# Second gated FFN with ScalarE, VectorE and GpSimd in written order instead of a scheduler's order

## The chip, the cores and the metric

The kernel runs on one NeuronCore of a Trainium2 chip. The metric is the device time of one execution in microseconds: 1541.91 us, the median of three runs (1540.91 to 1547.6). A profiled execution of the same kernel took 1539.89 us, of which the profile's span (first to last instruction) covers 1538.1 us.

## The reference

Three stages follow each other. The changed part is the last one.

```python
xread = softmax(x @ state.T / 8) @ state          # attention between 512 tokens and 32 states
sread = softmax(state @ x.T / 8) @ x              # per batch (8) and head (8), D = 64
x = concat([xread, sread]) -> rows of 512         # 8 * 544 = 4352 rows
x = ((x @ w1) * (x @ w2)) @ w3 @ w_out            # first FFN, 512 -> 1024 -> 512
out = (sigmoid(x @ w_gate) * (x @ w_val)) @ w_out2  # second FFN, 512 -> 1536 -> 512
```

The weights come as float64. The kernel reads their 32-bit words and builds float32 from them on the chip. Each float32 operand of a matrix product is split into a high part (rounded to the matmul's reduced fp32 format) and a low part (the rest), and three of the four cross products are summed.

## The kernel before

Everything up to `ffn1(B, ...)` (L633) is attention and the first FFN; its result goes to DRAM as `yd`, transposed, in five pieces of 7, 7, 7, 7 and 6 blocks of 128 rows. Then the pools are released and the second FFN starts.

The second FFN runs 15 steps: three passes over the hidden width (four tiles of 128 columns each, `JQ`), and in each pass the five row pieces. A step consists of two calls of `gate_val` (the halves q = 0 and q = 1), and the step's `down` product (hidden to 512 columns) runs inside the next step, so 14 + 14 products and one `down` belong to each step.

- `gate_val` computes gate and value with a fast 2x2 block scheme that needs 7 products in place of 8. Each of the 14 products (7 for gate, a = 0; 7 for value, a = 1) is six matmuls of 448 columns (384 in the piece of 6 blocks) into one PSUM bank. Tags: A (two banks, accumulated over products 1, 6, 5, 3 and read out in between to `s1`, `u2`, `u4` by ScalarE, `keep_`), B (two banks), C (one bank, product 2). `finish` adds a kept piece (VectorE), applies the sigmoid (ScalarE, gate) or multiplies gate and value (VectorE), and splits the product into `p` (high part on ScalarE, low part on VectorE).
- `down` runs, per block of 128 rows, twelve matmuls of 512 columns `po<-wo,p`, and evicts to `ob`; in passes 1 and 2 it adds the partial result `pr` of the pass before, read back from DRAM.
- `load_y` brings in the operands of the next step: per half of the 512 inputs two loads `yf`, four differences `yt`, seven splits into the 14 pairs `y` (high part ScalarE, low part VectorE). Sixteen pairs of buffers exist.
- `prep_next` prepares the weights of the next pass beside this work: 24 pieces per pass are loaded (`raw`, DMA issued by GpSimd), narrowed from float64 (`narrow`: two operations on ScalarE, four on VectorE), combined on GpSimd, split (`o`: ScalarE, then GpSimd), and stored to DRAM (`wd`, `wod`; GpSimd's queue, 36 stores per pass). Loads and store tiles share two buffers (tag `io`).

Only TensorE's order is written out by hand (L143). The other engines' instructions are put in order by a list scheduler, from a priority that follows the program text and from its own cost estimates; each engine then executes that order strictly, so an instruction that waits holds back all that stands behind it on its engine. `prep_step` hands the scheduler one piece of weight work per product (L833, L841) or per block of `down` (L856).

Of the kernel before, what the change touches and what calls it, by code (L numbers as in the profile page):

```python
# [20 lines left out]
def tile_state_attention__then__gated_ffns(  # L21
# [19 lines left out]
    nc = tc.nc  # L41
# [27 lines left out]
    def cvt(src, cv, nb=3):  # L69

        raw = cv.tile([P, 512, 2], U32, name="raw", bufs=nb)
        shape = list(src.shape)
        view = raw if len(shape) == 2 else raw.rearrange("p (k f) t -> p k f t", k=shape[1])
        flat = "p f t -> p (f t)" if len(shape) == 2 else "p k f t -> p k (f t)"
        nc.sync.dma_start(out=view.rearrange(flat), in_=src)  # L80
        m = cv.tile([P, 512], F32, name="m", bufs=nb)
        narrow(raw, m, cv.tile([P, 512], I32, name="r", bufs=2))
        return m

    def narrow(raw, m, r):
        hi, lo = raw[:, :, 1], raw[:, :, 0]
        mu = m.bitcast(U32)
        nc.scalar.activation(out=m, in_=hi.bitcast(F32), func=AF.Abs)  # L88
        nc.scalar.activation(out=r, in_=lo, func=AF.Copy, scale=2.0**-29)  # L89
        nc.vector.tensor_scalar_max(m, m, 2.0**-15)  # L90
# [52 lines left out]
    with tc.manual_schedule(engines={mybir.EngineType.PE}):  # L143
# [413 lines left out]

        ys = {}

        def load_y(c, cv):  # L560

            n = blocks[c] * P // 2
            ys[c] = [[None, None] for _ in range(7)]
            for kb in range(2):
                raw = []
                for h in range(2):
                    r = cv.tile([P, 2, 448 if cv is p2.get("c2") else 512], F32, tag="raw", name="yf", bufs=3)
                    nc.sync.dma_start(
                        out=r[:, :, :n], in_=y_d[c][2 * h + kb].rearrange("p (c n) -> p c n", c=2)
                    )  # L570
                    raw.append(r)
                b11, b12, b21, b22 = (r[:, i, :n] for r in raw for i in range(2))
                tt = [
                    cv.tile([P, 448 if cv is p2.get("c2") else 512], F32, tag="m", name="yt", bufs=3)[:, :n]
                    for _ in range(3)
                ]
                t1, t2, t3 = tt
                nc.vector.tensor_tensor(out=t1, in0=b12, in1=b11, op=ALU.subtract)
                nc.vector.tensor_tensor(out=t2, in0=b22, in1=t1, op=ALU.subtract)
                nc.vector.tensor_tensor(out=t3, in0=b22, in1=b12, op=ALU.subtract)  # L580
                t4 = b12
                nc.vector.tensor_tensor(out=t4, in0=b21, in1=t2, op=ALU.subtract)
                for o, v in enumerate((b11, t2, t3, t1, b21, b22, t4)):
                    t = [
                        p2["c1"].tile([P, 448], F32R, name=f"y{i}", bufs=16)[:, :n] for i in range(2)
                    ]
                    split(t[0], t[1], v)
                    ys[c][o][kb] = t
# [43 lines left out]
        slots[4].append(lambda: load_y(0, cv))  # L632
# [14 lines left out]
        p2["c2"] = c2  # L647
# [25 lines left out]
        def prep_next(ps):  # L673

            def load(src, k=None):
                raw = c2.tile([P, 256, 2], U32, tag="io", name="raw2", bufs=2)
                if k is None:
                    nc.gpsimd.dma_start(out=raw.rearrange("p f t -> p (f t)"), in_=src)  # L680
                else:
                    nc.gpsimd.dma_start(
                        out=raw.rearrange("p (k f) t -> p k (f t)", k=k), in_=src
                    )
                m = c2.tile([P, 256], F32, name="m2", bufs=4)
                narrow(raw, m, c2.tile([P, 256], I32, name="r2"))
                return m

            def put(dst, v):
                t = c2.tile([P, 2, 256], F32R, tag="io", name="o2", bufs=2)  # L690
                split(t[:, 0], t[:, 1], v, sub=nc.gpsimd)
                nc.gpsimd.dma_start(out=dst, in_=t.bitcast(F32))

            def chain(jp, a):
                m = {}
                j0 = 2 * jp
                dst = w_d[j0 + a].rearrange("p (o i f) -> o p i f", o=7, i=2)

                def get(jj, kb):
# [3 lines left out]
                    m[jj, kb] = load(w.rearrange("(k p) f -> p k f", p=P), k=2)  # L703

                def diff(o, x0, x1, op=ALU.subtract):
                    nc.gpsimd.tensor_tensor(out=o, in0=x0, in1=x1, op=op)

                def s1():
                    m["s"] = c2.tile([P, 256], F32, name="sm2")
                    diff(m["s"], m[1, 0], m[1, 1], ALU.add)  # L710
                    put(dst[2], m[1, 1])

                def s3():
                    put(dst[3], m["s"])
                    diff(m[1, 0], m[0, 0], m[1, 0])

                def s2():
                    put(dst[5], m[1, 0])
                    diff(m["s"], m["s"], m[0, 0])

                def s4():
                    put(dst[4], m["s"])
                    diff(m["s"], m[0, 1], m["s"])

                wo = wo_d[j0 + a].rearrange("p (i f) -> p i f", i=2)

                def out_half(h):
                    w = w_out2[(j0 + a) * P : (j0 + a + 1) * P, h * 512 : (h + 1) * 512]
                    m["o", h] = load(w)

                return [
                    lambda: get(1, 0), lambda: get(1, 1), lambda: get(0, 0), s1, s3,
                    lambda: get(0, 1), s2, lambda: put(dst[0], m[0, 0]), s4,
                    lambda: put(dst[1], m[0, 1]), lambda: put(dst[6], m["s"]),
                    lambda: out_half(0), lambda: put(wo[:, :, :256], m["o", 0]),
                    lambda: out_half(1), lambda: put(wo[:, :, 256:], m["o", 1]),
                ]

            return [chain(ps * 2 + q, a) for q in range(2) for a in range(2)] + [[]]

        todo2 = []

        def prep_step():
            if todo2:
                todo2.pop(0)()


        OPS = {1: (0, 0), 6: (4, 1), 7: (5, 2), 5: (3, 3), 2: (1, 4), 3: (6, 5), 4: (2, 6)}

        def gate_val(ps, c, q, between):  # L750
# [6 lines left out]
            def product(a, k, o, start):  # L757
                w, xx = OPS[k]
                w = wt[q, a][:, w]
# [22 lines left out]
            def finish(a, jj, cc, o, what):  # L782

                if a == 0:
                    t = c2.tile([P, 448], F32, name=f"sg{jj}{cc}")[:, :n]
                    if what is not None:
                        nc.vector.tensor_tensor(out=t, in0=o, in1=kept[a, what], op=ALU.add)  # L787
                        o = t
                    nc.scalar.activation(out=t, in_=o, func=AF.Sigmoid)  # L789
                    sg[jj, cc] = t  # L790
                    return
                t = sg[jj, cc]
                if what is not None:
                    nc.vector.tensor_tensor(out=kept[a, what], in0=o, in1=kept[a, what], op=ALU.add)  # L794
                    o = kept[a, what]
                nc.vector.tensor_tensor(out=t, in0=o, in1=t, op=ALU.mult)  # L796
                p = pt[2 * jp + jj]
# [140 lines left out]
```

## Time and profile before

| | before |
|---|---|
| median of three runs | 1541.91 us |
| profiled execution: time, span | 1539.89 us, 1538.1 us |
| busy in the span: TensorE, VectorE, ScalarE, GpSimd | 1380.0, 939.3, 748.1, 341.2 us |
| matmuls of the second FFN: first start, last end | 651.05 us, 1528.64 us |
| busy 722.5 to 1155.1 us: TensorE, VectorE, ScalarE | 386.99, 267.73, 205.41 of 432.6 us |
| busy 1155.1 to 1511.4 us: TensorE, VectorE, ScalarE | 351.44, 204.53, 132.82 of 356.3 us |

[...] A row of the timeline merges neighbouring instructions of one kind. The brackets give the idle time in front of it and what ended that. Buffer numbers are left out, so `raw2`, `m2`, `o2`, `s1`, `u2` of the code read `raw`, `m`, `o`, `s`, `u`.

### The profile page before, as it was taken

How to read it: one execution, taken by the hardware profiler on the slowest of the kernel's cores; microseconds unless marked ns; L12 is line 12 of the kernel's file. 1: busy time of each engine (PE TensorE's matmuls, PEld its weight loads, DVE VectorE, ACT ScalarE, POOL GpSimd, SP SyncE). 2: the span in 40 equal slices, each digit the busy share in tenths (PEclk: the TensorE clock that was granted, in tenths of full speed). 3: DMA queues.
4: the chain of work that ended last, by engine and by line, in shares of the span. 5: the costliest groups of instructions: out<-in, count | busy, mean ns of one | idle time of the engine just before them, and what ended most of it. 6: DMA issues, size and time to landing. Idle time of an engine off the chain costs nothing. (4 is left out here: it accounts for less than half of the span.)

```text
span 1538.1 us, 19065 instructions
## 1 busy us (share of the span) xinstructions
PE 1380.0 (90%) x6560; PEld 1160.7 (75%) x6560; DVE 939.3 (61%) x1639; ACT 748.1 (49%) x1480; POOL 341.2 (22%) x375
## 2 busy tenths in 40 slices
PE   5668999996999999859998998798989999999997
PEld 3347777774777878847787787687878888888886
DVE  7799767677745245328567466384674566457543
ACT  6666656755545445336446445263452354235321
POOL 2352123346412210032431422323310000000000
PEclk8789999998999999969999999899999999999999
DMA  8767647858523212462433338435433374341322
GB/s 259 249 183 205 177 156 220 255 187 260 186 82 96 62 61 80 166 269 94 166 133 103 130 136 305 174 117 177 159 104 107 132 267 157 98 128 57 107 96 69
DMA packets 155304, 237.18 MB, mean 154 GB/s; under 512 B 46920, under 2 KB 99656, under 8 KB 153160
## 3 DMA queue, kind: packets, MB, share of 16 engines
q1 hardware_dynamic: 132936, 169.38, 34.9%
q0 software_dynamic: 10752, 40.90, 7.6%
q10 hardware_dynamic: 11520, 25.70, 4.6%
q8 instruction: 51, 0.84, 0.2%
q14 instruction: 45, 0.37, 0.1%
HBM read 150.99 MB, written 84.93 MB: 153 GB/s over the span
## 5 line engine op out<-in xcount | busy, mean ns | idle before, releaser
L763 PE MATMUL psA<-y,wt 128*128 128x448 f32 (+1 forms) x1440 | 319.9, 371 | 39.0 <-ACT s L61 21.8
L763 PEld LDWEIGHTS psA<-y,wt 128*128 128x128 f32 x1440 | 273.6, 194 | 67.8 <-ACT s L61 28.0
L849 PE MATMUL po<-wo,p 128*128 128x512 f32 x1224 | 282.7, 391 | 2.2 <-ACT ob L61 1.9
L849 PEld LDWEIGHTS po<-wo,p 128*128 128x128 f32 x1224 | 230.4, 189 | 51.0 <-ACT ob L61 2.5
L763 PE MATMUL psB<-y,wt 128*128 128x448 f32 (+1 forms) x720 | 166.3, 367 | 16.9 <-DVE u L794 16.9
L109 PE MATMUL pab<-aT,swh 128*128 128x512 f32 x512 | 149.5, 415 | 23.0 <-ACT asb L61 12.3
L90 DVE TENSOR_SCALAR m<-m 128x512 f32<-128x512 f32 (+1 forms) x116 | 63.2, 549 | 159.5 <-ACT m L88 152.4
L763 PEld LDWEIGHTS psB<-y,wt 128*128 128x128 f32 x720 | 137.0, 193 | 28.5 <-DVE u L794 18.4
L67 POOL TENSOR_TENSOR swh<-swf,swh 128x512 fp32r<-128x512 f32 x64 | 89.4, 1399 | 241.9 <-ACT swh L61 225.1
L109 PEld LDWEIGHTS pab<-aT,swh 128*128 128x128 f32 x512 | 97.2, 197 | 48.5 <-ACT asb L61 14.5
L109 PE MATMUL py<-u,wp 128*128 128x512 f32 (+1 forms) x576 | 131.0, 380 | 0.0
L864 DVE TENSOR_TENSOR ob<-po,pr 128x512 f32<-128x512 f32 x68 | 46.8, 690 | 127.2 <-PE po L849 115.3
L109 PEld LDWEIGHTS py<-u,wp 128*128 128x128 f32 x576 | 103.4, 188 | 26.1 <-issue 6.4
L88 ACT ACTIVATE m<-raw 128x512 f32<-128x512 f32 (+1 forms) x116 | 65.9, 570 | 116.8 <-DMA raw<-in_moe_w_out 51.3
L431 DVE TENSOR_TENSOR asb<-asb,pab 128x512 f32<-128x512 f32 (+1 forms) x72 | 47.1, 655 | 102.3 <-PE pab L112 90.3
L763 PE MATMUL psC<-y,wt 128*128 128x448 f32 (+1 forms) x360 | 84.3, 370 | 18.4 <-DVE s L794 18.3
L61 ACT ACTIVATE p<-sg 128x448 fp32r<-128x448 f32 (+1 forms) x120 | 66.9, 563 | 58.9 <-DVE sg L796 57.9
L763 PEld LDWEIGHTS psC<-y,wt 128*128 128x128 f32 x360 | 67.0, 192 | 28.4 <-DVE s L794 24.2
L89 ACT ACTIVATE r<-raw 128x512 int32<-128x512 uint32 (+1 forms) x116 | 65.7, 566 | 44.0 <-DVE m L98 26.5
L789 ACT ACTIVATE sg<-psA 128x448 f32<-128x448 f32 (+1 forms) x30 | 15.7, 522 | 144.3 <-PE psA L763 144.3
L61 ACT ACTIVATE u<-psA 128x448 f32<-128x448 f32 (+1 forms) x120 | 63.0, 527 | 44.2 <-PE psA L763 43.1
L95 DVE SCALAR_TENSOR_TENSOR m<-raw,m 128x512 uint32<-128x512 uint32 (+1 forms) x116 | 81.6, 709 | 1.8
(128 smaller groups left out, 2194.5 us busy)
## 6 DMA issues: line engine op xcount, KB each, us to landing
raw<-in_moe_w SPq DMA_DIRECT2D x48, 512.0 KB, 5.1
yf<-yd SPq DMA_DIRECT2D x48, 448.0 KB, 3.5
wt<-wd SPq DMA_DIRECT2D x12, 1792.0 KB, 10.2
part<-ob SPq DMA_DIRECT2D x68, 256.0 KB, 2.0
pr<-part SPq DMA_DIRECT2D x68, 256.0 KB, 3.0
swd<-swst ACTq DMA_DIRECT2D x32, 512.0 KB, 3.8
swf<-swd SPq DMA_DIRECT2D x128, 128.0 KB, 3.0
wd<-o POOLq DMA_DIRECT2D x56, 256.0 KB, 3.0
```

What stands on the lines that cost most here:

```text
L61: nc.scalar.activation(out=o, in_=i, func=AF.Copy)
L67: (sub or nc.vector).tensor_tensor(out=lo, in0=src, in1=hi.bitcast(F32), op=ALU.subtract)
L88: nc.scalar.activation(out=m, in_=hi.bitcast(F32), func=AF.Abs)
L89: nc.scalar.activation(out=r, in_=lo, func=AF.Copy, scale=2.0**-29)
L90: nc.vector.tensor_scalar_max(m, m, 2.0**-15)
L95: nc.vector.scalar_tensor_tensor(out=mu, in0=hi, scalar=0xC0000000, in1=mu, op0=ALU.bitwise_and, op1=ALU.bitwise_or)
L109: nc.tensor.matmul(o, w[i], xx[k], start=n == 0 and i + k == 0, stop=False)
L431: nc.vector.tensor_tensor(out=asb[:, :n], in0=asb[:, :n], in1=pab[1][:, :n], op=ALU.mult)
L763: nc.tensor.matmul(o, w[:, i, kb * P : (kb + 1) * P], xx[kb][h], start=start, stop=i == 1 and kb == 1, skip_group_check=True,)
L789: nc.scalar.activation(out=t, in_=o, func=AF.Sigmoid)
L849: nc.tensor.matmul(o, pt[j][i][:, s * P : (s + 1) * P], wot[j][:, h], start=j == js[0] and i + h == 0, stop=j == js[-1] and i == 1,)
L864: nc.vector.tensor_tensor(out=ob, in0=o, in1=pr, op=ALU.add)
```

## The change

ScalarE, VectorE and GpSimd join TensorE in written order for the second FFN. TensorE's `gate_val` order stays, except that `down` now stands after three products of the first half and not after eight.

- A counter `now` goes up by one at every product and every half block of `down` (`begin`). Work that follows a product is put a fixed number of slots behind it (`later`): sigmoid and high parts two slots, low parts three.
- Token work (`next_tokens`, in place of `load_y`) is a list of 22 pieces with a condition each on the slot; `fill` hands out at most two splits per slot as long as a budget of VectorE time is positive.
- Weight work (`next_weights`, in place of `prep_next`) is a list of pieces handed out at least 2.0 us (of the planner's own clock) apart, from 10 us on. Its loads and stores are issued by ScalarE's queue instead of GpSimd's: the load of a piece at least 4.0 us ahead of its conversion, the store two slots behind the split. `raw2` gets one buffer of its own, `o2` two, `m2` three; the eight halves of `w_out2` tiles come last in a pass.
- The row `pr` of the next block is loaded one block ahead, and the pool's tiles are laid out in another order (four names more are allocated ahead of the weight tiles `wt`).

```diff
+        def later(k, cost, fn):
+            due.setdefault(clock["now"] + k, []).append((cost, fn))
+        def begin(length):
+            clock["now"] += 1
+            clock["us"] += length
+            clock["vector"] = min(clock["vector"] + length, 2.5)
+            for cost, fn in due.pop(clock["now"], []):
+                vector(cost)
+                fn()
+        def fill(quiet):
+            act = 0
+            if prep and clock["us"] >= clock["prep"]:
+                if not prep[0][0] or (
+                    quiet and clock["vector"] > -1.0 and clock["us"] >= clock["load"]
+                ):
+                    clock["prep"] = clock["us"] + 2.0
+                    act = 1
+                    clock["vector"] -= 1.5 * prep[0][0]
+                    for fn in prep.pop(0)[1:]:
+                        fn()
+            while tokens and clock["vector"] > 0.5 and act < 2 and tokens[0][0]():
+                _, is_split, fn = tokens.pop(0)
+                if is_split:
+                    act += 1
+                else:
+                    vector()
+                fn()
...
+                    copy("act", y[0], v)
+                    later(1, 0.62, lambda: (minus(y[1], v, y[0].bitcast(F32)), ready.add((c, o, kb))))
...
+            def load(src, k):
+                raw = c2.tile([P, 256, 2], U32, name="raw2")
+                nc.scalar.dma_start(out=raw.rearrange("p (k f) t -> p k (f t)", k=k), in_=src)
+                raws.append(raw)
+                clock["load"] = clock["us"] + 4.0
+            def conv(key):
+                raw = raws.pop()
+                m[key] = c2.tile([P, 256], F32, name="m2", bufs=3)
+                r = c2.tile([P, 256], I32, name="r2")
+                bits_act(raw, m[key], r)
+                later(1, 0.0, lambda: bits_vector(raw, m[key], r))
+            def put(dst, key):
+                t = c2.tile([P, 2, 256], F32R, name="o2", bufs=2)
+                split(t[:, 0], t[:, 1], m[key], sub=nc.gpsimd)
+                later(2, 0.0, lambda: nc.scalar.dma_start(out=dst, in_=t.bitcast(F32)))
...
                     nc.vector.tensor_tensor(out=t, in0=o, in1=kept[a, what], op=ALU.add)
+                    vector()
+                    later(2, 0.0, lambda: nc.scalar.activation(out=t, in_=t, func=AF.Sigmoid))
...
-                split(p[0][:, cc * n : (cc + 1) * n], p[1][:, cc * n : (cc + 1) * n], t)
+                later(2, 0.0, lambda: copy("act", hi, t))
+                later(3, 0.62, lambda: minus(lo, t, hi.bitcast(F32)))
...
-            for a, k in (
-                (0, 1), (1, 1), (0, 2), (0, 6), (1, 6), (0, 7), (0, 5), (1, 5),
-            ):
+            for a, k in ((0, 1), (1, 1), (0, 2)):
                 step(a, k)
-                if q:
-                    prep_step()
             between()
...
+        ordered = {mybir.EngineType.Activation, mybir.EngineType.DVE, mybir.EngineType.Pool}
+        with tc.manual_schedule(engines=ordered):
```

ScalarE at the start of the second FFN, the kernel before and then the changed one (`s`, `u` are read-outs of bank A, `m`, `r`, `o` weight work, `sg` the sigmoid):

```order
L88 ACTIVATE m_6218<-raw_6216 128x256
L89 ACTIVATE r_6219<-raw_6216 128x256
L88 ACTIVATE m_6237<-raw_6235 128x256
L89 ACTIVATE r_6238<-raw_6235 128x256
L61 ACTIVATE o_6275<-m_6237 128x256
L88 ACTIVATE m_6257<-raw_6255 128x256
L89 ACTIVATE r_6258<-raw_6255 128x256
L61 ACTIVATE o_6287<-sm_6273 128x256
L61 ACTIVATE s_6082<-psA 128x448
L61 ACTIVATE o_6320<-m_6218 128x256
```

```order
L61 ACTIVATE s_6016<-psA 128x448
L61 ACTIVATE s_6025<-psA 128x448
L61 ACTIVATE u_6046<-psA 128x448
L920 ACT_TABLE_LOAD
L920 ACTIVATE sg_6034<-sg_6034 128x448
L61 ACTIVATE u_6055<-psA 128x448
L61 ACTIVATE u_6070<-psA 128x448
L61 ACTIVATE u_6080<-psA 128x448
L920 ACTIVATE sg_6072<-sg_6072 128x448
L791 DMA raw_6090<-in_moe_w_gate 128x2x256
```

Before, eight operations of weight work that need landed loads stand ahead of the first read-out; in the changed kernel six read-outs and two sigmoids come first, and only then is the first weight load issued.

SP at the end of the first FFN, before and changed, with the semaphores that each DMA waits for (a `DMA...` semaphore is an earlier transfer; `wt`, `wo` are the second FFN's weights):

```order
L659 DMA wt_5981<-wd 128x3584 [waits DMASW0_49,PE_49]
L659 DMA wt_5983<-wd 128x3584 [waits DMAHW5_49,DMASW2_49]
L668 DMA wo_5985<-wod 128x1024 [waits DMAHW6_49,DMASW1_49,DVE_49]
L668 DMA wo_5987<-wod 128x1024 [waits DMAHW7_49,DMASW3_49,DVE_49]
L668 DMA wo_5989<-wod 128x1024 [waits DMAHW0_49,DMASW5_49]
```

```order
L711 DMA wt_5985<-wd 128x3584 [waits DMASW0_49]
L711 DMA wt_5987<-wd 128x3584 [waits DMAHW5_49,DMAHW6_49,DMASW2_49,DMAHW7_49,DVE_49,PE_49]
L720 DMA wo_5989<-wod 128x1024 [waits DMASW1_49,PE_49]
L720 DMA wo_5991<-wod 128x1024 [waits DMASW3_49]
L720 DMA wo_5993<-wod 128x1024 [waits DMAHW0_49,DMASW5_49,PE_49]
```

The first weight tile no longer waits for TensorE; the TensorE event of the second one lies 136 matmuls before the end of the first FFN (a `pab` product), where before the first tile waited for one that lies 20 before it (`py`).

VectorE in the second half of a step of pass 0, before and changed (`u`, `sg`: `finish` of the value; `yt`, `y`: token work):

```order
L794 TENSOR_TENSOR u_7482<-psB,u_7482 128x448
L582 TENSOR_TENSOR yf<-yf,yt 128x448
L67 TENSOR_TENSOR y_7050<-yt,y_7049 128x448
L67 TENSOR_TENSOR y_7054<-yt,y_7053 128x448
L67 TENSOR_TENSOR y_7058<-yt,y_7057 128x448
L67 TENSOR_TENSOR y_7062<-yf,y_7061 128x448
L796 TENSOR_TENSOR sg_7463<-u_7482,sg_7463 128x448
L67 TENSOR_TENSOR y_7066<-yf,y_7065 128x448
L67 TENSOR_TENSOR y_7070<-yf,y_7069 128x448
```

```order
L577 TENSOR_TENSOR y_7339<-yt,y_7338 128x448
L918 TENSOR_TENSOR sg_7354<-psB,u_7352 128x448
L924 TENSOR_TENSOR u_7362<-psB,u_7362 128x448
L927 TENSOR_TENSOR sg_7354<-u_7362,sg_7354 128x448
L577 TENSOR_TENSOR y_7377<-yf,y_7376 128x448
L577 TENSOR_TENSOR y_7389<-yt,y_7388 128x448
L577 TENSOR_TENSOR y_7392<-yt,y_7391 128x448
L577 TENSOR_TENSOR yt<-yf 128x448
L577 TENSOR_TENSOR yt<-yf,yt 128x448
L927 TENSOR_TENSOR sg_7394<-psA,sg_7394 128x448
```

Before, runs of token work stand inside a value's add and multiply; in the changed kernel the two stand next to each other and at most five token operations in a row stand between read-outs. From one add of bank C to the next (14 products) the fullest half has 23 tensor operations and one conversion of four on VectorE.

## Rows read from the trace of the kernel before

**Rows 1.** Busy time and granted clock by stretch (us, busy and count per engine, PEclk, DMA).
```profile
645.50:722.50 77.00, 51.34 (x217) 43.86 (x218) 39.26 (x81) 35.37 (x75) 21.17 (x29) 0.82 0.56 217
1155.10:1511.40 356.30, 351.44 (x1706) 315.02 (x1706) 204.53 (x364) 132.82 (x270) 0.00 (x0) 1.00 0.37 124
```
**Rows 2.** Waits of PE, 645 to 1538 us: in total, times, longest.
```profile
PE psA L763 <- ACT s L61: 21.8, 14, 7.8
PE psC L763 <- DVE s L794: 18.3, 15, 4.2
PE psB L763 <- DVE u L794: 16.9, 4, 9.0
```
**Rows 3.** Timeline of PE at the start of the second FFN.
```profile
644.36 1.12 PE L112 MATMUL py<-u,wp 128*128 128x256 f32 x8
651.05 2.61 PE L763 MATMUL psA<-y,wt 128*128 128x448 f32 x6 [5.57 <-DMA wt<-wd]
657.07 2.61 PE L763 MATMUL psA<-y,wt 128*128 128x448 f32 x6 [3.41 <-DMA wt<-wd]
```
**Rows 4.** Timeline and waits of SP, 615 to 660 us.
```profile
643.12 0.81 SPq L659 DMA_DIRECT2D wt<-wd  x2
...
SPq L659 <- PE py L109: 16.9, 1, 16.9
```
**Rows 5.** Chain that ended last, in order of time: pieces of pass 2.
```profile
1259.39 16.32 PE po L849 x72
...
1296.48 2.14 DVE y L67 x4
...
1306.86 1.22 PE psB L763 x6
...
1310.51 19.07 PE po L849 x84
...
1494.90 1.04 PE psC L763 x6
```
**Rows 6.** Timeline of PE: `down` of step 0, of step 7, the last.
```profile
722.47 16.48 PE L849 MATMUL po<-wo,p 128*128 128x512 f32 x72
...
1155.12 19.25 PE L849 MATMUL po<-wo,p 128*128 128x512 f32 x84
...
1513.92 14.72 PE L849 MATMUL po<-wo,p 128*128 128x512 f32 x63 [0.29 <-ACT p L61]
```
**Rows 7.** Timeline of ACT, then of PE, in step 6.
```profile
1058.03 0.43 ACT L88 ACTIVATE m<-raw 128x256 f32<-128x256 f32 x1 [5.87 <-DMA raw<-in_moe_w_out]
...
1059.44 2.61 PE L763 MATMUL psB<-y,wt 128*128 128x448 f32 x6 [3.91 <-DVE u L794]
```
**Rows 8.** ACT at the first two read-outs: timeline.
```profile
666.27 0.53 ACT L61 ACTIVATE s<-psA 128x448 f32<-128x448 f32 x1
...
676.73 0.53 ACT L61 ACTIVATE s<-psA 128x448 f32<-128x448 f32 x1
```
**Rows 9.** Instructions on the tile `raw`, 640 to 1200 us: who waited, landing times.
```profile
ACT m L88: 101.4, 35
...
DMA to landing us min/median/max: 2.8/3.4/10.3
```
**Rows 10.** The same for the tile `o`.
```profile
L67 POOL TENSOR_TENSOR o<-m,o x48: 717/736/2160, 659.9 to 1132.6; 128x256 fp32r<-128x256 f32 x48
...
ACT o L61: 70.5, 26
...
DMA to landing us min/median/max: 2.3/2.8/7.1
```
**Rows 11.** A DMA issued by ScalarE (first FFN), duration ns min/median/max.
```profile
L453 ACTq DMA_DIRECT2D yd<-ysb x48: 326/326/1496, 190.6 to 645.9; - x48
```
**Rows 12.** Timeline of DVE: first and last operation of one conversion.
```profile
675.25 0.29 DVE L90 TENSOR_SCALAR m<-m 128x256 f32<-128x256 f32 x1 [8.85 <-ACT m L88]
...
676.47 0.43 DVE L98 CUSTOM_DVE_ANT_0 m<-m,r 128x512 uint16<-128x512 uint16 x1
```
**Rows 13.** DVE by form, 700 to 980 us, then 1200 to 1460 us.
```profile
L67 DVE TENSOR_TENSOR p<-sg,p 128x448 fp32r<-128x448 f32 x28 | 17.5, 636 | 1.4 <-ACT p L61 1.2
...
L67 DVE TENSOR_TENSOR p<-sg,p 128x448 fp32r<-128x448 f32 x31 | 18.7, 619 | 6.5 <-ACT p L61 6.1
```

More of the change, by code (lines that the diff above doesn't have):

```diff
@@ L558, in tile_state_attention__then__gated_ffns, with y_tiles, y_raw @@
         ys = {}
-        def load_y(c, cv):
+        def y_tiles(n):
+            return [p2["c1"].tile([P, 448], F32R, name=f"y{i}", bufs=16)[:, :n] for i in range(2)]
+        def y_raw(c, kb, h, pool, w):
             n = blocks[c] * P // 2
-            ys[c] = [[None, None] for _ in range(7)]
-            for kb in range(2):
[L565 to L586, printed above, removed]
@@ L646, in tile_state_attention__then__gated_ffns, with vector @@
         tc.swap_default_side()
-        p2["c2"] = c2
+        clock = {"now": 0, "us": 0.0, "vector": 0.0, "prep": 10.0, "load": 0.0}
+        due = {}
+        tokens = []
+        prep = []
+        half = {}
+        ready = {(0, o, kb) for o in range(7) for kb in range(2)}
+        def later(k, cost, fn):
+            due.setdefault(clock["now"] + k, []).append((cost, fn))
+        def vector(cost=0.62):
+            clock["vector"] -= cost
+        def begin(length):
[23 more added lines that the diff above has]
+                fn()
         pt = {}
@@ L671, in load_wo @@
                 wot[j] = t
[L673 to L699, printed above, removed]
+        OPS = {1: (0, 0), 6: (4, 1), 7: (5, 2), 5: (3, 3), 2: (1, 4), 3: (6, 5), 4: (2, 6)}
@@ L702, in get @@
                     ]
-                    m[jj, kb] = load(w.rearrange("(k p) f -> p k f", p=P), k=2)
-                def diff(o, x0, x1, op=ALU.subtract):
-                    nc.gpsimd.tensor_tensor(out=o, in0=x0, in1=x1, op=op)
+                    step(lambda: conv(key), w.rearrange("(k p) f -> p k f", p=P), 2)
                 def s1():
-                    m["s"] = c2.tile([P, 256], F32, name="sm2")
-                    diff(m["s"], m[1, 0], m[1, 1], ALU.add)
-                    put(dst[2], m[1, 1])
@@ L725, in chain @@
[L725 to L748, printed above, removed]
+                    put(d[0], 11)
+                    comb("s", 12, "s")
+                get(21)
+                get(22)
+                step(s1)
+                step(lambda: put(d[3], "s"))
+                get(11)
@@ L750, in gate_val @@
+            for q in range(2):
+                for a in range(2):
+                    group(2 * (ps * 2 + q), a)
+            weights = len(out)
+            for j in range(ps * JQ, (ps + 1) * JQ):
+                for h in range(2):
+                    output(j, h)
+            clock["out"] = len(out) - weights
+            return out
         def gate_val(ps, c, q, between):
@@ L758, in product @@
                 w, xx = OPS[k]
+                assert (c, xx, 0) in ready and (c, xx, 1) in ready
                 w = wt[q, a][:, w]
```

229 lines of the change are left out of this document (175 added, 54 removed).

## The prediction

> **What bounds the kernel now.** I read the busy time by stretch first, then TensorE's waits, then the timeline of the places they name. In the second FFN TensorE is the engine with the most work, but unevenly: in the last pass it is busy 351.4 of 356.3 us at full granted clock, while in the first 77 us it is busy 51.3 us at a mean clock of 0.82 [rows 1]. So the question is how far each stretch lies above what its matmuls take back to back. A product of 448 columns takes 1.215 us (the rows say 1.22, two take 2.43), one of 384 columns 1.04 us, a `down` of seven blocks 19.07 us, of six blocks 16.32 us [rows 5]. A step of seven blocks is then 28 x 1.215 + 19.07 = 53.1 us, of six blocks 28 x 1.04 + 16.32 = 45.4 us. Twelve of the first and three of the second are 773.4 us.
>
> The stretch that holds them runs from the end of the first FFN, 644.36 + 1.12 = 645.5 us [rows 3], to the last `down`'s end, 1513.92 + 14.72 = 1528.6 us [rows 6]: 883.2 us. So 109.8 us are lost. The starts of `down` [rows 6] cut the loss in three:
> - 645.5 to 722.5 us: 77.0 us for 36 products (43.7 us). Lost: 33.3 us.
> - 722.5 to 1155.1 us, steps 1 to 7: 432.7 us for 364.0 us of matmuls. Lost: 68.7 us, 9.8 us a step. Here the weights of the next pass are prepared beside the products.
> - 1155.1 to 1528.6 us, steps 8 to 14 and the last `down`: 373.5 us for 365.7 us. Lost: 7.8 us, about 1.1 a step. Token work is the same here, weight work is gone.
>
> The waits say who held TensorE: ScalarE's read-out of bank A (21.8 us in 14 waits), VectorE's release of bank C (18.3 us in 15) and of bank B (16.9 us in 4) [rows 2]. Behind those stand transfers. ScalarE sat 5.87 us for a weight load in step 6, VectorE's additions came late, and TensorE's next product then waited 3.91 us at half clock, 2.61 us for six matmuls [rows 7]. ScalarE sat 101.4 us in 35 waits for weight loads [rows 9] and 70.5 us in 26 waits for store buffers [rows 10]. That is the loss of steps 1 to 7: waits for DMAs on ScalarE, in front of read-outs that were ready.
>
> **The change, part by part.**
>
> *Start.* The first two products waited 5.57 and 3.41 us for the weight tiles `wt` [rows 3], because SP sat 16.9 us for a `py` matmul and issued both at 643.1 us [rows 4]. After the change the first tile waits for none of TensorE's work, so it can go when SP became free, 643.1 - 16.9 = 626.2 us; the second waits for a matmul 136 before the end of the first FFN, at 0.12 us each [rows 3] about 645.5 - 16.3 = 629.2 us. Before, both had landed 657.07 - 643.12 = 14.0 us after issue, with weight loads beside them. At the same pace they are in at 643.2 us, ahead of the first product. The third and fourth wait goes too: the first read-outs ran at 666.3 and 676.7 us [rows 8], behind the eight operations of weight work that the order shows, and now stand first. Tiles for the second half (14 products later, at 662.5 us) are issued around 645 us; they need 14 us at the old pace and would arrive at 659. I take 1 us of loss in place of 33.3; the bounds are 0 and the old DMA waits, 9.0 us.
>
> *Steps 1 to 9.* Weight work stays the same in amount (48 loads, 72 stores over two passes), but it moves. GpSimd's 120 DMA issues go to ScalarE's queue, 0.33 us each [rows 11]: 39 us over ten steps, on an engine that was busy about half of the time and that has read-outs with a reserve of two products (2.43 us) each. I cost it at nothing; the cover is that reserve. The two kinds of wait are pulled apart: a load is issued at least 4.0 us of the plan ahead, where the median landing is 3.4 us [rows 9], and a store has the two slots to its issue plus 2.8 us [rows 10], 5.2 us, before its buffer is wanted by the next split but one, some 4.9 us later. So most waits vanish, and those left are short: up to a few tenths each on stores, longer where a landing runs to 7 or 10 us (the ends in rows 9 and 10). What is queued behind a waiting DMA issue on ScalarE is the next read-out, and TensorE is behind that once 2.43 us are used up.
> VectorE is late next. In the fullest half it has 23 tensor operations at 0.535 us (four in 2.14) [rows 5] and one conversion of 1.65 us [rows 12], together 14.0 us in 14 products of 17.0 us. That leaves 18% free, and bank C, read 4 slots before it is wanted, has that as cover.
> Bounds for a step: 0 and the old 9.8 us. The nearest rows are steps 8 to 14 with 1.1 us, where only token work ran; I take 1.2, so 9 x 1.2 = 10.8 us.
>
> *Ends of passes.* The weight tiles `wt` are loaded there beside weight loads. Two ends at 2 us each, 4 us; bounds 0 and 10 (the longest landing of a load, once per end, half hidden).
>
> *Steps 10 to 14 and the last `down`.* 6 x 1.0 = 6 us, bounds 0 and 7.8. `pr` one block ahead gains nothing, since TensorE has three `po` banks. `down` after three products gives VectorE's token work the 19 us of `down` before the fourth product; that is inside the 1.0.
>
> **Sum.** 645.5 + 773.4 + 1 + 10.8 + 4 + 6 = 1440.7 us for the end of TensorE. Behind it stay 1538.1 - 1528.6 = 9.5 us to the span's end and 1539.9 - 1538.1 = 1.8 us around it: 1452 us. The profiled execution lies 2.0 us below the median of the runs, so the forecast for the median is 1454 us.
>
> **The rivals.**
> - *A: ScalarE still blocks on DMAs, half as bad.* For it: ScalarE now carries the issues too, and an issue also waits for GpSimd's subtraction. Against it: two buffers of its own for stores and the load ahead. If the old 61 waits return at their old mean of (101.4 + 70.5) / 61 = 2.8 us and only what exceeds the reserve of 2.43 us counts, that is 24 us; with the wt loads 6 more: 1454 + 30 = 1484 us.
> - *B: VectorE becomes the bound in the second halves.* At its full duration of 0.63 us per operation [rows 13] the fullest half takes 23 x 0.63 + 1.65 = 16.1 us, still under 17.0. It needs GpSimd's help: four of its operations stand in such a half, 0.74 us each [rows 10]. If each held VectorE up fully, the half would take 19.1 us, 2.1 us over, in nine steps 19 us: 1473 us. Against it: with GpSimd working VectorE's splits took 636 ns, without it 619 [rows 13]; GpSimd's own reached 2160 ns against a least of 717 [rows 10].
>   [...]
> - *C, slower: the fixed order turns every weight DMA into a stall of TensorE.* Place: ScalarE's 120 DMA issues. The pieces follow each other two slots apart, so a block of 2.8 us eats the reserve of the next one as well, and in written order nothing is moved ahead of it. At 2.8 us for each of the 120 the stalls are 336 us at most; at 1.0 us each the time is 1454 + 120 = 1574 us. It decides from 88 / 120 = 0.73 us per DMA. Against it: the plan's distances above, and that landings in the quiet steps are near the median.
> - *D: nothing is gained in steps 1 to 7*, because the list scheduler's order was as good and the waits come from the transfers themselves. Then only the start is gained, 33 us: 1509 us. Against it: TensorE loses 1.1 us a step as soon as weight work is gone, with the same scheduler.
>
> **How the numbers follow.** The forecast has 0.70, A 0.12, B 0.07, C 0.05, D 0.06. The forecast's bounds are all losses at zero, 645.5 + 773.4 + 11.3 + 2 = 1432 us, and some 3 us a step, 1470. The range takes in A and B: 1436 to 1492 us. Half a per cent of this kernel, 8 us, is about what can be told from no change. Faster by more than that holds for all but C and part of D: 0.93; within it 0.02; slower 0.05.
>
> **What would show it.** Right: the first `psA` product at 645 to 647 us without a wait for `wt`; the starts of `down` 53 to 55 us apart from the first steps on; TensorE's waits for ScalarE and VectorE together under 20 us; granted clock 1.00 through the second FFN; ScalarE's waits on `raw` and `o` each much shorter than 2.8 us. Wrong: steps of 56 us and more with waits of ScalarE for `raw` or `wd` in front of read-outs (A, C), or VectorE busy through and bank C released late (B); a late first product would be the start's term alone, worth up to 9 us.

## The result and the profile after

| | before | after |
|---|---|---|
| median of the runs | 1544.76 us (1540.91 to 1549.66, 4 runs) | 1461.16 us (1458.15 to 1464.57, 4 runs) |
| profiled execution: time, span | 1539.89, 1538.1 us | 1458.15, 1456.4 us |
| first to last matmul of the second FFN | 651.05 to 1528.64 us | 643.62 to 1447.51 us |

The ratio is 0.9458, 95% interval 0.942 to 0.9496. The forecast was 1454 us; the range of 1436 to 1492 us holds the result.

In the profile PE is TensorE, DVE VectorE, ACT ScalarE, POOL GpSimd and SP an engine that issues DMAs here; PEclk is the clock granted to TensorE as a share of full speed.

The second FFN's TensorE work is now nearly back to back. By stretch (columns as in [rows 1]; before the first `down`, then to the tenth, then to the last):

```profile
643.60:681.30 37.70, 37.70 (x188) 34.95 (x187) 24.34 (x44) 21.30 (x42) 3.33 (x3) 1.00 0.58 216
681.30:1172.60 491.30, 474.94 (x2257) 420.94 (x2257) 366.28 (x686) 254.09 (x558) 89.51 (x101) 0.99 0.51 175
1172.60:1430.30 257.70, 255.57 (x1232) 228.34 (x1232) 152.42 (x268) 100.05 (x200) 0.00 (x0) 1.00 0.35 112
```

TensorE's timeline, at the ends of these stretches:

```profile
642.66 1.12 PE L116 MATMUL py<-u,wp 128*128 128x256 f32 x8
643.62 2.60 PE L891 MATMUL psA<-y,wt 128*128 128x448 f32 x12
...
681.32 4.95 PE L989 MATMUL po<-wo,p 128*128 128x512 f32 x21
...
1172.62 3.58 PE L989 MATMUL po<-wo,p 128*128 128x512 f32 x15
...
1432.70 14.82 PE L989 MATMUL po<-wo,p 128*128 128x512 f32 x64 [0.42 <-DVE p L577]
```

The first product follows the first FFN without a wait; before, two waited 5.57 and 3.41 us [rows 3]. With the prediction's durations the three stretches cost 31 products = 37.7 us, 465.3 us and 270.4 us (to the last matmul's end). So 0, 26.0 and 4.5 us are lost, 30.5 us in place of 109.8 us.

The 26.0 us are not spread evenly. From the start of one `down` to the next, less the back-to-back time, steps 1 to 9 lose 1.6, 2.0, 0.6, 1.9, 8.0, 2.0, 0.9, 3.2 and 5.9 us: more than half stands in steps 5 and 9. The starts of `down` in steps 5, 6 and 9 (the one in step 10 is the row at 1172.62 us above), 58.3 us apart for 50.3 us of matmuls and 54.6 us for 48.7 us:

```profile
894.88 11.07 PE L989 MATMUL po<-wo,p 128*128 128x512 f32 x48
...
953.23 6.96 PE L989 MATMUL po<-wo,p 128*128 128x512 f32 x30
...
1118.04 2.24 PE L989 MATMUL po<-wo,p 128*128 128x512 f32 x9
```

SP's timeline: the first two `wt` are issued from 624.70 us on, where before SP sat for a `py` until 643.12 us [rows 4].

```profile
624.70 4.22 SPq L711 DMA_DIRECT2D wt<-wd  x2
...
647.54 0.80 SPq L711 DMA_DIRECT2D wt<-wd  x2
```

TensorE's waits from 640 to 1460 us (total, times, longest) have one large entry, where before there were three [rows 2]:

```profile
PE psA L891 <- ACT u L61: 14.9, 9, 4.0
PE po L989 <- DVE ob L1005: 2.1, 4, 1.2
```

The nine are one in each of steps 1 to 9, always just after `down`: product (0, 5) needs bank A, which ScalarE still has to read out after product (0, 6).

ScalarE's waits for `raw` and for `o`, 640 to 1200 us (who waited: us, times), fell from 101.4 and 70.5 us [rows 9, 10]:

```profile
  ACT m L89: 12.9, 5
...
DMA to landing us min/median/max: 2.4/2.9/9.3
```

```profile
L67 POOL TENSOR_TENSOR o<-m,o x72: 727/742/1205, 675.3 to 1141.3; 128x256 fp32r<-128x256 f32 x72
...
  ACT o L61: 8.2, 7
...
DMA to landing us min/median/max: 2.0/2.4/5.3
```

But a wait that the prediction did not speak of became ScalarE's longest for a transfer: the splits of token work, for the rows `yf`. ScalarE's waits, 640 to 1460 us:

```profile
ACT y L61 <- DMA yf<-yd: 64.9, 16, 7.0
```

In the kernel before ScalarE had no wait for `yf`, and VectorE had 5.0 us in 5 times. In e_sched below, the changed text under the list scheduler, ScalarE waits 57.6 us in 21 times: these waits came with the changed text, not with the written order.

Two places show how it reaches TensorE. In step 9 the timeline of SP, then of ScalarE, then of TensorE reads:

```profile
1129.51 0.32 SPq L1008 DMA_DIRECT2D part<-ob  x1
...
1130.80 0.51 SPq L1008 DMA_DIRECT2D part<-ob  x1
1131.36 1.03 SPq L571 DMA_DIRECT2D yf<-yd  x2
...
1137.34 0.58 ACT L61 ACTIVATE y<-yf 128x448 fp32r<-128x448 f32 x1 [7.02 <-DMA yf<-yd]
...
1140.76 0.42 ACT L61 ACTIVATE o<-m 128x256 fp32r<-128x256 f32 x1 [2.19 <-DVE m L102]
...
1143.11 0.87 ACT L61 ACTIVATE u<-psA 128x384 f32<-128x384 f32 x2 [1.93 <-POOL o L67]
...
1143.65 3.73 PE L891 MATMUL psA<-y,wt 128*128 128x384 f32 x12 [3.22 <-ACT u L61]
```

`yf` is issued at 1131.36 us, behind stores of finished rows, and ScalarE has reached its split 1.0 us before. It sits 7.02 us; a conversion, a split and a store that were due in the meantime follow, and only then the read-out. In step 5 it is a split and then a conversion (ScalarE, then TensorE):

```profile
911.18 0.37 ACTq L791 DMA_DIRECT2D raw<-in_moe_w_gate  x1
...
914.79 0.58 ACT L61 ACTIVATE y<-yf 128x448 fp32r<-128x448 f32 x1 [2.21 <-DMA yf<-yd]
...
918.90 0.43 ACT L89 ACTIVATE m<-raw 128x256 f32<-128x256 f32 x1 [2.70 <-DMA raw<-in_moe_w_gate]
...
919.55 0.96 ACT L61 ACTIVATE u<-psA 128x448 f32<-128x448 f32 x2
...
920.13 4.85 PE L891 MATMUL psA<-y,wt 128*128 128x448 f32 x12 [4.00 <-ACT u L61]
```

Twelve matmuls took 4.85 us after that wait, twice their 2.43 us: the granted clock from 920.1 to 925.0 us was 0.50.

### The profile page after: what moved, and what is told of

Its sections match the earlier page's. It is cut to its first block, busy times and chain, and to the rows that moved or that the text cites. A ratio compares the mean times of both kernels' runs of the same rounds, so it can differ in the third digit from the quotient of the medians.

```text
span 1456.4 us, 19117 instructions
## 1 busy us (share of the span) xinstructions
PE 1356.2 (93%) x6560; PEld 1150.0 (79%) x6560; DVE 970.2 (67%) x1639; ACT 750.1 (52%) x1480; POOL 281.3 (19%) x255
## 5 line engine op out<-in xcount | busy, mean ns | idle before, releaser
L891 PE MATMUL psA<-y,wt 128*128 128x448 f32 (+1 forms) x1440 | 308.5, 363 | 15.2 <-ACT u L61 14.9
L891 PEld LDWEIGHTS psA<-y,wt 128*128 128x128 f32 x1440 | 268.6, 190 | 37.7 <-ACT u L61 19.2
L113 PE MATMUL pab<-aT,swh 128*128 128x512 f32 x512 | 148.6, 413 | 23.4 <-ACT asb L61 13.3
L891 PE MATMUL psB<-y,wt 128*128 128x448 f32 (+1 forms) x720 | 161.9, 360 | 0.0
L67 POOL TENSOR_TENSOR o<-m,o 128x256 fp32r<-128x256 f32 x72 | 62.5, 869 | 427.5 <-ACT o L61 393.7
L113 PEld LDWEIGHTS pab<-aT,swh 128*128 128x128 f32 x512 | 96.7, 196 | 48.5 <-ACT asb L61 15.5
L577 DVE TENSOR_TENSOR y<-yf,y 128x448 fp32r<-128x448 f32 (+1 forms) x112 | 68.7, 638 | 48.8 <-ACT y L61 48.8
L61 ACT ACTIVATE y<-yf 128x448 fp32r<-128x448 f32 (+1 forms) x120 | 62.9, 557 | 65.2 <-DMA yf<-yd 64.9
L90 ACT ACTIVATE r<-raw 128x512 int32<-128x512 uint32 (+1 forms) x116 | 65.8, 568 | 34.6 <-DVE m L102 14.8
L116 PE MATMUL pab<-aT,swh 128*128 128x512 f32 x256 | 82.4, 404 | 0.7 <-POOL swh L67 0.6
```

What stands on the lines that cost most here:

```text
L61: nc.scalar.activation(out=o, in_=i, func=AF.Copy)
L67: (sub or nc.vector).tensor_tensor(out=lo, in0=src, in1=hi.bitcast(F32), op=ALU.subtract)
L113: nc.tensor.matmul(o, w[i], xx[k], start=n == 0 and i + k == 0, stop=False)
L116: nc.tensor.matmul(o, w[1 - late], xx[late], start=False, stop=n == len(pairs) - 1)
L577: nc.vector.tensor_tensor(out=o, in0=x0, in1=x1, op=ALU.subtract)
L891: nc.tensor.matmul(o, w[:, i, kb * P : (kb + 1) * P], xx[kb][h], start=start, stop=i == 1 and kb == 1, skip_group_check=True,)
```

## The experiments

TensorE's order is the same in the changed kernel and in all that derive from it. Loss is the time above the back-to-back sums in the profiled execution: up to the first `down`, to the tenth, to the end. The last column is TensorE's waiting for read-outs of bank A (`u`, `s`) by ScalarE, us / times.

| run | median us | ratio to before, 95% | loss | wait |
|---|---|---|---|---|
| changed kernel | 1461.2 | 0.9458 [0.942, 0.9496] | 0, 26.0, 4.5 | 14.9 / 9 |
| e_lay | 1539.5 | 0.9946 [0.9927, 0.9965] | below | |
| e_sched | 1508.4 | 0.9727 [0.968, 0.9773] | 30.7, 37.0, 1.7 | 39.4 / 13 |
| e_act | 1454.3 | 0.9393 [0.9367, 0.942] | 0.9, 18.7, 2.9 | 9.5 / 9 |
| e_pool | 1468.6 | 0.9504 [0.9472, 0.9536] | 0, 31.7, 4.4 | 16.9 / 9 |
| e_io | 1488.9 | 0.9639 [0.9617, 0.966] | 0, 55.0, 4.8 | 34.2 / 19 |
| e_load0 | 1456.9 | 0.941 [0.9392, 0.9428] | 2.4, 16.6, 5.6 | 4.3 / 5 |
| e_quiet | 1458.2 | 0.942 [0.9406, 0.9434] | 0, 22.0, 4.8 | 11.7 / 6 |
| e_wait | 1442.8 | 0.9321 [0.9307, 0.9335] | 0, 15.9, 1.2 | 6.9 / 3 |
| e_sp | 1443.7 | 0.9334 [0.9316, 0.9352] | 0, 9.6, 3.2 | 3.7 / 3 |
| e_wa | 1448.0 | 0.9372 [0.9346, 0.9398] | 0.9, 15.5, 2.3 | 5.5 / 4 |
| e_sa | 1445.9 | 0.9355 [0.9329, 0.9382] | 1.1, 10.6, 3.0 | 5.0 / 4 |
| e_all | 1450.1 | 0.9379 [0.9366, 0.9392] | 2.8, 17.1, 1.2 | 3.0 / 4 |

**The start: layout or order?** e_lay is the kernel before, with the changed layout of the pool alone:

```diff
-            ("sg11", 1, 448), ("s1", 2, 448), ("u2", 2, 448), ("u4", 2, 448),
+            ("sg11", 1, 448), ("io", 2, 512), ("m2", 4, 256), ("sm2", 1, 256), ("r2", 1, 256),
+            ("s1", 2, 448), ("u2", 2, 448), ("u4", 2, 448),
```

> The kernel before (list scheduler, weight DMAs on GpSimd) with one edit: four names (io, m2, sm2, r2) get their place in the pool ahead of s1, as in the changed kernel, so that the first weight tile wt waits for none of TensorE's work and the second for a matmul 136 before the end of the first FFN. Theory 1, the two waits for wt are only 9 of the 33.3 us lost at the start, the rest is weight work that stands ahead of the first read-outs: the start of the first down moves by 0 to 12 us and the time is 1530 to 1545 us. Theory 2, the early wt loads alone give the start: it moves by 20 to 33 us, 1510 to 1525 us.

Theory 1 held: 1539.5 us, and the first `down` at 715.65 us, 6.8 us earlier. The timelines of SP and TensorE show the two `wt` early, no wait for them, and another wait in their place:

```profile
628.06 4.38 SPq L659 DMA_DIRECT2D wt<-wd  x2
...
646.98 2.60 PE L763 MATMUL psA<-y,wt 128*128 128x448 f32 x12
...
665.06 2.61 PE L763 MATMUL psA<-y,wt 128*128 128x448 f32 x6 [14.27 <-ACT s L61]
```

From 646.98 us to the first `down` are 68.7 us for 36 products (43.7 us): 25.0 us remain of 33.3.

**What the written order is worth.** e_sched has the changed kernel's text but leaves all engines but TensorE to the list scheduler:

```diff
-        ordered = {mybir.EngineType.Activation, mybir.EngineType.DVE, mybir.EngineType.Pool}
+        ordered = {mybir.EngineType.PE}
```

> The changed kernel's text (ScalarE issues the weight DMAs, separate buffers for loads and stores, pieces handed out by budget), but only TensorE in written order, so that the list scheduler orders ScalarE, VectorE and GpSimd again. Theory 1, the order earns the gain of steps 1 to 9: the scheduler puts weight work in front of read-outs again, TensorE's waits for ScalarE and VectorE grow from the changed kernel's 18 us to over 50 us, and the time is 1500 to 1545 us. Theory 2, the buffers, the early loads and the queue earn it, whatever the order: 1455 to 1470 us, as the changed kernel (1461 us).

1508.4 us is theory 1's time, but the gain lies elsewhere than it said. The text without the order takes 2.7% off, the order the other 2.7% (0.9458 / 0.9727 = 0.972). The start falls back by 30.7 us, near the 25.0 us that e_lay had left. ScalarE's timeline there, then TensorE's:

```profile
648.58 0.43 ACT L89 ACTIVATE m<-raw 128x256 f32<-128x256 f32 x1 [7.02 <-DMA raw<-in_moe_w_gate]
...
653.02 0.43 ACT L89 ACTIVATE m<-raw 128x256 f32<-128x256 f32 x1 [3.69 <-DMA raw<-in_moe_w_gate]
...
656.80 0.54 ACT L61 ACTIVATE s<-psA 128x448 f32<-128x448 f32 x1 [1.23 <-POOL o L67]
...
657.40 2.61 PE L891 MATMUL psA<-y,wt 128*128 128x448 f32 x6 [12.61 <-ACT s L61]
```

The scheduler puts two conversions, each waiting for its load, ahead of the first read-out. In steps 1 to 9 it loses 37.0 us, 11 more than the changed kernel, while the kernel before lost about 71 (the same sum, up to the `down` at 1259.39 us [rows 5]). So in steps 1 to 9 the text took off more than the order, and the order's main gain is the start. TensorE's waits for ScalarE and VectorE came to 47.6 us, not over 50. The profiled execution (1494.9 us) was the shortest of four, by 13.5 us under their median, so the usual losses are larger; where, no profile shows.

e_act keeps the written order on ScalarE alone (`ordered = {mybir.EngineType.Activation}`).

> The changed kernel's text with ScalarE in written order only; the list scheduler orders VectorE and GpSimd (and TensorE). With the scheduler on all three the time was 1508 us, with none of them 1461 us. Theory 1, ScalarE's order is what counts, since the waits stood there: 1461 to 1475 us. Theory 2, an order that only one engine keeps is worth little, since what ScalarE waits for is then placed by the scheduler elsewhere: 1490 to 1520 us.

1454.3 us, under the ranges of both theories and next to theory 1: the order of ScalarE is all that the change needed of the order. Written order on VectorE and GpSimd added nothing; the changed kernel, which has it, is if anything slower (the intervals of the ratios touch at 0.942).

**The parts of the text.** e_pool puts the 120 weight DMAs back on GpSimd's queue (`nc.scalar.dma_start` to `nc.gpsimd.dma_start` in `load` and `put`).

> The changed kernel with its 48 weight loads and 72 weight stores back on GpSimd's queue, the order of all else kept. Theory 1, the queue is worth nothing beside the order: 39 us of issues leave ScalarE, but none of them held a read-out; 1456 to 1466 us. Theory 2, the queue matters: a store behind GpSimd's own subtractions and a load behind a store that waits come late, ScalarE waits for them, and the time is over 1475 us. Theory 3, the issues on ScalarE are part of what steps 1 to 9 still lose (26 us): 1440 to 1452 us.

1468.6 us lies between theories 1 and 2: some 7 us slower by the ratios, whose intervals overlap (5.6 us in the second FFN of the profiles). The rows of the tile `o` show a store's issue on GpSimd longer than on ScalarE, 560 ns against 327 ns (medians), and it follows GpSimd's own operations:

```profile
L805 POOL DMA_DIRECT2D wd<-o x56: 557/560/665, 679.5 to 1079.1; - x56
```

e_io lets weight loads and stores share two buffers again, all else as changed:

```diff
-                raw = c2.tile([P, 256, 2], U32, name="raw2")
+                raw = c2.tile([P, 256, 2], U32, tag="io", name="raw2", bufs=2)
-                t = c2.tile([P, 2, 256], F32R, name="o2", bufs=2)
+                t = c2.tile([P, 2, 256], F32R, tag="io", name="o2", bufs=2)
```

> The changed kernel, but weight loads and store tiles share two buffers again (tag io), as in the kernel before; the order, the queue and the lead stay. Theory 1, the buffers of their own are the part of the text that counts: a load then waits for a store to land and a store tile for a conversion, ScalarE's waits for raw and for o grow from 21 us to over 80 us, TensorE's waits for ScalarE from 15 us to over 40 us, and the time is 1480 to 1510 us. Theory 2, at 2 us between pieces two buffers are enough once the order is fixed: 1456 to 1470 us.

1488.9 us, theory 1. The store waits are back (ScalarE's waits, then TensorE's); those for `raw` are not (8.1 us in 4), and TensorE's waits for the read-outs rose to 34.2 us, not over 40:

```profile
ACT o L61 <- DMA wd<-o: 77.8, 33, 4.3
...
PE psA L891 <- ACT u L61: 32.4, 17, 5.5
```

e_load0 takes away the lead of 4.0 us:

```diff
-                clock["load"] = clock["us"] + 4.0
+                clock["load"] = clock["us"]
```

> The changed kernel without the lead of 4.0 us that the planner keeps between a weight load and its conversion (the conversion follows as soon as the planner's 2.0 us are over). Theory 1, the lead is what removed ScalarE's waits for raw: at a median landing of 2.4 to 3.4 us each of the 48 conversions then waits a few us, ScalarE's waits for raw grow from 13 us in 5 to over 60 us, and the part beyond the reserve of 2.4 us reaches TensorE; 1475 to 1500 us. Theory 2, the read-outs' reserve covers a missing lead: 1456 to 1466 us.

Theory 1 fell. ScalarE's waits for `raw` rose as it said in kind, from 12.9 us in 5 to 30.0 us in 19, and TensorE waited less. Who waited for `raw`:

```profile
  ACT m L89: 30.0, 19
```

and TensorE's waits:

```profile
PE psA L891 <- ACT u L61: 4.3, 5, 2.0
```

1456.9 us is theory 2, 4 us under the changed kernel, with intervals that overlap. More waiting of ScalarE for `raw` went with less waiting of TensorE; that these waits fell where a read-out has two products to spare is argued, not shown. ScalarE's waits for `yf` did not fall either, and yet steps 1 to 9 lose only 16.6 us:

```profile
ACT y L61 <- DMA yf<-yd: 71.3, 19, 6.8
```

Not taken apart are the earlier `down` in TensorE's order, `pr` one block ahead, the budget and the 2.0 us between pieces. And each of these three runs keeps the written order, so none shows what its part is worth under the list scheduler.

**What steps 1 to 9 still lose.** e_quiet hands out no conversion at the two products after a `down` (`(0, 6), (1, 6)` join the products left out in `fill`).

> The changed kernel, but the planner hands out no conversion of a weight piece at the product (0, 6), the first after a down, nor at (1, 6). There ScalarE's read-out u of bank A is wanted after one product, and the changed kernel lost 14.9 us in nine waits for it. Theory 1, weight work stands in front of that read-out: the nine waits shrink to under 5 us and the time is 1446 to 1456 us (the run without a lead of 4.0 us, whose pieces fall on other products, already showed 4.3 us there and 1457 us). Theory 2, ScalarE is late there from the waits for yf before and during the down, wherever the conversions stand: 1458 to 1466 us.

1458.2 us is theory 2's, with 11.7 us of waits. Over all steps the conversions there are not the main thing; in step 5 alone the loss fell from 8.0 to 3.2 us, and it rose in others. e_wait starts token work on a new set of rows four slots after the last split of the set before:

```diff
+                    if (o, kb) == (6, 1):
+                        later(1, 0.0, lambda: clock.update(raw=clock["now"]))
...
-            begun = clock["now"] + 3
-            first = at(1) if clock["now"] == 0 else lambda: clock["now"] > begun
+            clock["raw"] = 1 << 30
+            first = at(1) if clock["now"] == 0 else lambda: clock["now"] > clock["raw"] + 4
```

> The changed kernel, but token work on a new set of rows starts four slots after the last split of the set before, in place of a fixed slot, so that ScalarE's splits y are handed out when yf can have landed. ScalarE waited 64.9 us in 16 times for yf. Theory 1, these waits are what makes ScalarE late for the read-outs after a down: they fall under 20 us, TensorE's waits for ScalarE under 6 us, and the time is 1444 to 1456 us. Theory 2, they lie in ScalarE's own idle time: they go and the time stays, 1457 to 1465 us. Theory 3, the splits are squeezed into fewer slots and down or the next step waits for y: over 1470 us.

Theory 1 in kind, and the time is a little better than it said: 1442.8 us, 1.4% under the changed kernel (0.9321 / 0.9458) and the fastest of all runs. The waits fell less than it said (under 20 and under 6 us). ScalarE's for `yf` halved, TensorE's for ScalarE too:

```profile
ACT y L61 <- DMA yf<-yd: 31.6, 7, 7.1
...
PE psA L893 <- ACT u L61: 6.9, 3, 3.9
```

Steps 1 to 9 lose 15.9 us in place of 26.0, and the last steps 1.2 in place of 4.5. Step 9 went from 5.9 to 1.2 us, step 5 stayed (8.4 us). The edit moves the splits' own work as well as their waits, so the two are not parted. e_sp adds SP in written order, each `yf` load written where its buffer comes free:

```diff
+                    later(1, 0.0, lambda: pend.pop((o, kb), lambda: freed.add((o, kb)))())
...
+                elif key in freed:
+                    get(*at_)
+                else:
+                    pend[key] = lambda at_=at_: get(*at_)
```

> As the run with the later token work, and in addition SP's DMAs in written order too, each load yf written where the buffer that it takes comes free, so that it is not issued behind stores and the reading back of pr that wait. Theory 1, the loads yf were late because of SP's order: ScalarE's waits for yf fall under 10 us and the time is 3 to 8 us below the run without this edit. Theory 2, the buffer is what comes free late (three buffers for four loads): within 3 us of that run. Theory 3, SP in written order blocks on its own waits and pr comes late: over 5 us slower.

1443.7 us, and 33.8 us of waits for `yf`: theory 2 in time. The place of the load on SP is not what is left. That its buffer is, is argued, not shown: no run has a fourth buffer.

**Together?** e_wa is e_wait with ScalarE alone ordered, e_sa is e_sp with ScalarE and SP alone ordered, and e_all is e_wait with the edits of e_quiet and e_load0.

> The later token work, with ScalarE alone in written order (VectorE and GpSimd by the list scheduler). The later token work took 18 us off the changed kernel, ScalarE alone in written order 7 us. Theory 1, they take away different losses (ScalarE waiting for yf; VectorE and GpSimd held in an order that ScalarE's delays pass on to) and add up in part: 1434 to 1441 us. Theory 2, both shorten the same wait, ScalarE's read-out after a down: 1441 to 1446 us, as with the later token work alone.

> The later token work with ScalarE and SP in written order, VectorE and GpSimd by the list scheduler. With SP in written order and all else as well the second FFN took 786.2 us from its first to its last matmul, 4 us less than without it (790.4), but the runs were no faster. Theory 1, those 4 us are real and lay behind a first FFN that ended 3 us later in that profile: 2 to 6 us below the run with ScalarE alone. Theory 2, they are chance: within 2 us of it.

> All three engines in written order, with the three edits that made it faster one by one: the later token work (1443 us), no conversions at the two products after a down (1458 us), no lead of 4.0 us (1457 us). With the later token work alone TensorE still lost 6.9 us in three waits for the read-out u after a down, and in front of one of them stood a conversion that waited 2.56 us for a load issued 7.5 us ahead. Theory 1, the edits take away different waits: these three go and the time is 1434 to 1441 us. Theory 2, they moved the same few waits, and without the lead ScalarE waits for raw elsewhere: 1441 to 1448 us.

None adds up. e_wa took 1448.0 us, above both theories and, by intervals apart, slower than e_wait. Of the 4.3 us between the two profiled executions 1.7 lie in the second FFN (792.1 against 790.4 us from first to last matmul); so that the written order of VectorE and GpSimd helps once ScalarE's large waits are gone is not shown. e_sa took 1445.9 us (1440.77 to 1447.13), 2.1 us under e_wa; that decides nothing. e_all took 1450.1 us, above both theories, and in kind theory 2: the read-out's waits fell to 3.0 us and others came (TensorE's waits, then ScalarE's and VectorE's timelines in step 5):

```profile
PE po L991 <- DVE ob L63: 4.6, 1, 4.6
PE psA L893 <- ACT u L61: 3.0, 4, 1.7
PE psC L893 <- DVE s L926: 2.2, 1, 2.2
```

```profile
906.89 0.43 ACT L89 ACTIVATE m<-raw 128x256 f32<-128x256 f32 x1 [7.04 <-DMA raw<-in_moe_w_gate]
...
907.42 0.29 DVE L94 TENSOR_SCALAR m<-m 128x256 f32<-128x256 f32 x1 [6.88 <-ACT m L89]
```

Without the lead the load of this piece went out at 897.29 us, while the next pass's `wt` (issued from 892.03 us on) were loading, and landed 9.6 us later. VectorE, in written order, waited behind ScalarE, and its eviction of `down` (at 910.17 us) was late.

## Why the prediction was right, and where it was off

- *Start, forecast loss 1 us.* Right: 37.70 us busy of 37.70. Its two causes are parted by e_lay and e_act: the early `wt` give about 8 us (33.3 to 25.0, and 8 us in the runs), the order of ScalarE the rest (e_act loses 0.9 us there, e_sched 30.7). The first two loads went out from 624.70 us on; the forecast had 626.2 and 629.2.
- *Steps 1 to 9 with the pass ends, forecast 10.8 + 4 = 14.8 us.* This is the mis-sized term: 26.0 us, of which 491.3 - 474.9 = 16.4 us idle and the rest matmuls that took longer than back to back. The mechanism (waits for DMAs on ScalarE go, its order stands) was right. The step that failed is "most waits vanish, and those left are short". It counted ScalarE's waits for weight DMAs and not those for the other transfers in the same queue of work: the splits of `yf`, at a fixed slot, 64.9 us in 16 waits. Taking about half of them away (e_wait) brings the term to 15.9 us. That this is near the forecast is in part luck: step 5 alone still loses 8.4 us, the other eight 7.5 us together, where the forecast had 1.2 us a step and 2 us for the end of a pass. In step 5, at the end of the first pass, ScalarE of the changed kernel spends 7.6 of its 12.9 us of waits for `raw`; loads issued from 880 to 953 us land after 5.7 us in the median, those before after 2.8. So the term for the pass ends was too small as well. Nor are the waits for `yf` the only lever: e_load0 has more of them and loses 16.6 us. Common to these kernels is that ScalarE is late at the read-out after a `down`; which work in front of it counts most is open.
- *The cover of two products, 2.43 us per read-out.* Right as a size, and used up where several waits stand in a row: 7.02, 2.19 and 1.93 us in step 9.
- *The lead of 4.0 us as the reason for few waits.* Wrong as a reason for the time: without it ScalarE waits more and the kernel is no slower (e_load0). The other half, buffers of their own, is right: sharing them costs 28 us (e_io).
- *GpSimd's issues moved at no cost.* Right as far as the runs tell; if anything a little was gained (e_pool).
- *Steps 10 to 14 and the last `down`, forecast 6 us.* 4.5 us; e_wait's 1.2 us suggests that these too were mostly `yf`, though TensorE waited there for VectorE's `ob` (2.1 us) and not for a read-out of bank A.
- *The rivals.* A (ScalarE blocks) came true in part: 14.9 us of waits where it had 24, in part behind another DMA than those it named (`yf`). D fell: e_sched, which differs from the changed kernel in the order alone, loses 11 us more in steps 1 to 9 and 30.7 at the start. But D's doubt about the order in the middle was half right, since the text alone took the loss in steps 1 to 9 from about 71 to 37.0 us. C fell: all of the loss in steps 1 to 9 is 26.0 / 120 = 0.22 us per weight DMA, and it needed 0.73. B did not decide, but its cause is there. VectorE's `p` subtractions, 700 to 980 us and 1200 to 1420 us (count, busy and mean ns):

```profile
L577 DVE TENSOR_TENSOR p<-sg,p 128x448 fp32r<-128x448 f32 x32 | 21.2, 662 | 0.9
...
L577 DVE TENSOR_TENSOR p<-sg,p 128x448 fp32r<-128x448 f32 x32 | 19.8, 619 | 0.9
```

That is 43 ns more beside weight work, where before it was 17 [rows 13]; TensorE waited 2.8 us for VectorE in all of the second FFN, so the fullest halves still had room for it.

The sum, redone with what was measured: the first product started at 643.6 us (1.9 us ahead of the forecast's 645.5), 773.4 us of matmuls, 30.5 us lost: 1447.5 us, then 8.9 us to the span's end and 1.8 us around it, 1458.2 us. The median of the runs lies 3.0 us above. The early start hides part of the 8.7 us by which the losses (21.8 us forecast) were too small.

Of the signs, the first product without a wait for `wt` came, and TensorE's waits for ScalarE and VectorE were 18.5 us, under 20. The even steps did not come in steps 5 and 9, nor the clock of 1.00 throughout: it was 0.99 in steps 1 to 9.

## What to carry to other kernels

An engine in written order must have each of its waits placed, those of all transfers it consumes, not only those of the edit at hand: list what the engine waits for, and hand out a consumer after its load can have landed (here `yf` was left out, 64.9 us in 16 waits). Keep the waits away from the read-out with the least reserve, since several short ones in a row before it add up (7.02, 2.19 and 1.93 us in step 9) and the total over the kernel says little (ScalarE's for `raw` were 12.9 us in the changed kernel and 30.0 us in e_load0, at 1461.2 and 1456.9 us). And order by hand first the engine that stands in front of the bound one; here that alone gave all that the order gave (1508.4 to 1454.3 us), beside what the changed text gave before it (1545 to 1508).

## What was not expected of the hardware

Where an operation of VectorE and one of GpSimd overlapped in the changed kernel, the one that began later mostly took longer. From 690 to 1150 us, 47 of VectorE's SBUF adds and subtracts (128x448, those that stand alone in the timeline) began while a GpSimd operation ran; they took 0.97 us on average, where those beside none took 0.62 us. However early they began, 44 of the 47 ended 0.47 to 0.49 us after the GpSimd operation. In 19 cases VectorE was first; its own took 0.62 us, and GpSimd's, 0.74 us when it ran alone, 0.98 us. One pair (VectorE, GpSimd):

```profile
770.59 1.16 DVE L577 TENSOR_TENSOR p<-sg,p 128x448 fp32r<-128x448 f32 x1
...
770.51 0.76 POOL L67 TENSOR_TENSOR o<-m,o 128x256 fp32r<-128x256 f32 x1 [0.67 <-ACT o L61]
```

The prediction judged rival B by a mean over all `p`, of which most meet no GpSimd operation: in the kernel before, 2 of the 28 from 700 to 980 us [rows 13] do.

The end of the first FFN, which no edit changes, lay between 641.1 and 647.7 us in the profiles of these kernels, so differences of 5 us and less between single profiles are read here from the second FFN alone.
